# Attention and a two-layer network: matmul operands read alternately from two halves, an unmerged second layer, and a ninth pair transposed by TensorE

## The chip, the cores and the metric

The kernel runs on one core of a Trainium2 chip. The metric is the device time of one execution, in microseconds (us). The kernel before takes 996.13 us (median of three runs, 996.07 to 996.7).

## The reference, cut to what matters

There are 8 batches of 8 heads, 576 positions and 64 values per head. For each head a decayed causal attention is computed, the result is laid out as 4608 tokens of 512 values, and these go through two matrix products with a leaky rectifier between them.

```python
scores = scale * np.matmul(q, k.transpose(0, 1, 3, 2))
cum = np.cumsum(np.log(np.clip(f, 0.0001, 1.0)), axis=-1)
scores = np.where(causal, -1e9, scores + cum[:, :, :, None] - cum[:, :, None, :])
attn = np.exp(scores - scores.max(-1, keepdims=True))
attn = attn / (attn.sum(-1, keepdims=True) + 1e-09)
x = np.matmul(attn, v)            # then reshaped to (4608, 512)
h = x @ w_in                      # (4608, 2048)
g = np.maximum(h, 0.0) + alpha * np.minimum(h, 0.0)
return g @ w_out                  # (4608, 512)
```

## The kernel before, in words

**Order of the work.** The kernel describes its work as some thousands of small operations, each with an engine, an estimated duration, a key, the operations it depends on and the buffers it takes. `Plan.run` (line 136) then simulates the engines: it takes, again and again, the operation that can start first, ties by key, and emits its instructions. The order in each engine's queue is therefore what this planner made of the estimates. The estimates are short functions: `c_mm` (line 325) for one product of n columns, and others for ScalarE, VectorE and GpSimd. Each is multiplied by a random factor between 0.97 and 1.03, drawn from `SEED` (line 27). Attention has small keys and the first layer keys of a million and more, so products of the first layer fill what attention leaves free on TensorE.

**Split operands.** For accuracy most products are done on operands that are split into a high and a low part (type fp32r): high by high, high by low and low by high, three products into one bank, where a full fp32 product would be used otherwise. ScalarE copies the high part, and VectorE or GpSimd subtracts it from the original to get the low part. All products go through the helper `mm` (line 382), so line 383 stands for all of them in the profile; they are told apart by their tiles.

**Attention.** A pair is two heads; there are 32 pairs, 4 per batch. In the profile `Qhl` is the split query and key of a pair; the first four pairs use unsplit `rqk`. Query and key of a pair come from DRAM in one row of 640 + 576 words, made on the host. The exponentials have to be transposed before they are multiplied by the values. For the first `NX` = 8 pairs (line 35) the function `attention` (line 570) does this by TensorE transposes of 128 x 128 blocks (helper `blocks`, line 609) and evacuates them from PSUM. For the others the function `turned` (line 831) uses VectorE transposes of 32 x 32 blocks (line 908) and moves the blocks between partitions by twelve DMAs per pair, six on SP's queue and six on GpSimd's (line 949), and four ScalarE copies (line 946). The decay rows of the first kind of pair come by DMA from DRAM, those of the second kind by two VectorE transposes (lines 515, 517). `quotient` (line 1003) normalizes the result on GpSimd and splits it (lines 1019, 1020) into a block `xx` of the first layer: the first 512 positions of a batch. The last 64 positions of all batches are collected through DRAM (`xt`) as a ninth block.

**First layer.** `ffn1` (line 1046) multiplies: per block and per group of 128 hidden values, four slices of the contraction times three split products of 512 columns, 12 products; 9 x 16 x 12 = 1728. The weights `wi` are split early (`split64`, line 358), and the result goes through the rectifier and to DRAM (`hd`). Each block needs the four pairs of its batch.

**Second layer.** The 4608 tokens are 18 units of 256. `ffn2` (line 1277) computes a unit by a Strassen-like scheme, in which 7 products take the place of 8. The moving operands are split sums of weight quarters (`wot`; the last four of eight lie in the freed `wi`), the stationary ones split sums of the hidden values (`gh`, low parts at line 1321, three buffers). There are 8 slices of the contraction, taken two at a time as groups. For all units but the last (`wide`) three of the seven products are merged: one product of 512 columns takes the high part of the stationary operand against high and low part of the weights side by side, one of 256 takes the low part. Such a unit has 8 x 18 = 144 products and uses five banks; the last one has 8 x 21 = 168 products of 256 columns and four banks. At its end a unit is put together by VectorE adds (lines 1364 to 1371 and 1394) and one ScalarE copy, and stored.

Of the kernel before, what the change touches and what calls it, by code (L numbers as in the profile page):

```python
# [19 lines left out]
NP = H // 2  # L20
# [4 lines left out]
QW = 640  # L25
ZW = 9 * 128
SEED = 66
# [7 lines left out]
NX = 8  # L35
# [14 lines left out]
UNITS = (2, 3, 0, 4, 5, 1, 6, 7, 14, 8, 9, 15, 10, 11, 16, 12, 17, 13)  # L50
NEG = -1.0e30
# [166 lines left out]
def attention_moe(  # L218
# [106 lines left out]
    def c_mm(n):  # L325
        return max(110, 13.3 + 0.4175 * n)
# [4 lines left out]
    def c_row(n, m):  # L331
        return m * max(110, 13.3 + 0.4175 * n)
# [25 lines left out]
    def split64(tiles, src, whi, wlo, key, deps, bufs_out):  # L358
# [21 lines left out]
        return [op("DVE", c_dve(512), lambda: ve.tensor_tensor(wlo(), a().bitcast(F32), whi().bitcast(F32), ALU.subtract), key, [cp], [ba] + bufs_out)]  # L380

# [188 lines left out]
    def attention(n):  # L570
# [11 lines left out]
        nt_ = 3 if n >= NN else 4  # L582
        masks = [o_eye, o_tri] if n < NM else []
# [32 lines left out]
        def tail(st):  # L616
# [4 lines left out]
            for g in range(2):  # L621
# [3 lines left out]
                def prods(bS=bS, ks=ks):  # L625
                    for c, (q, k) in enumerate(terms):
                        mm(bS.t[:, :288], q()[:, 512:640], k()[:, ks], c == 0, c == len(terms) - 1 and not (g and n < NM))
                    if g and n < NM:
                        mm(bS.t[:, 224:288], identb, tri2, False, True)
# [57 lines left out]
        def stretch(tiles, st):  # L687
# [4 lines left out]
            def prods():  # L692
                for i, g, c0 in part:
                    w = 128 * i + 128
                    for c, (q, k) in enumerate(terms):
                        for h in range(2):
                            r = slice(64 * h, 64 * h + 64)
                            mm(bS[g][h].t[:, c0 : c0 + w], q()[r, 128 * i : 128 * i + 128], k()[r, 0:w], c == 0, c == len(terms) - 1 and n >= NM)
# [132 lines left out]
    def turned(n):  # L831
# [22 lines left out]
        def score(i, h, out):  # L854
            r, w = slice(64 * h, 64 * h + 64), 128 * (i + 1)
            return [lambda c=c, q=q, k=k: mm(out(), q()[r, 128 * i : 128 * i + 128], k()[r, 0:w], c == 0, c == 2) for c, (q, k) in enumerate(terms)]
# [63 lines left out]
        def run2():  # L920
            for c0, c1, out in part:
                for c, (q, k) in enumerate(terms):
                    mm(out(), q()[:, 512:640], k()[:, c0:c1], c == 0, c == 2)
# [79 lines left out]
    def quotient(n, bxs, bri, deps, st):  # L1003
# [4 lines left out]
        def scaled():  # L1008
# [10 lines left out]
        xh = op("ACT", c_acs(512), lambda: ac.activation(bx.t[:, 0], bxs.t[:, 0:512], AF.Copy), st, [mu], [bxs, bx])  # L1019
        xl = op("POOL", c_po(512), lambda: po.tensor_tensor(  # L1020
            bx.t[:, 1], bxs.t[:, 0:512], bx.t[:, 0].bitcast(F32), ALU.subtract), st, [xh], [bxs, bx])
# [24 lines left out]
    def ffn1(b):  # L1046

        for fc in range(NF):
            bh, bs = Buf(rH), Buf(rhs)
            last = None  # L1050
            for half in range(2):
                def prods(bh=bh, fc=fc, half=half):
                    for c in (2 * half, 2 * half + 1):
                        x = x_ops[b, c][0].t
                        for k, (wt, m) in enumerate(((0, 0), (0, 1), (1, 0))):
                            mm(bh.t, wi[:, fc, wt, c], x[:, m], c + k == 0, c == NC4 - 1 and k == 2)
# [101 lines left out]
    wot = [None] * (NW - NV) + [wid[:, WN * i : WN * i + WN].rearrange("p (j k n) -> p j k n", k=2, j=7) for i in range(NV)]  # L1158

    def change():  # L1160
# [11 lines left out]
        for i in range(NW - NV):  # L1172
            wot[i] = p1.tile([128, 7, 2, 256], F32R, name=f"wot{i}")
# [33 lines left out]
    for c in range(NC4):  # L1207
        bx = Buf(rx)
        xh = op("ACT", c_acs(512), lambda c=c, bx=bx: ac.activation(bx.t[:, 0], tv()[:, c], AF.Copy), 1e4, [ld[c // 2]], [bt_, bx])
        xl = op("DVE", c_dve(512), lambda c=c, bx=bx: ve.tensor_tensor(  # L1210
            bx.t[:, 1], tv()[:, c], bx.t[:, 0].bitcast(F32), ALU.subtract), 1e4, [xh], [bt_, bx], two=True)
# [10 lines left out]
    def load_w_out(c):  # L1222
# [40 lines left out]
        for j0, j1, d in ((0, 3, done), (3, 7, [su])):  # L1263
            n = 256 * (j1 - j0)
            h = op("ACT", c_acs(n), lambda j0=j0, j1=j1: ac.activation(wot[c][:, j0:j1, 0], bx.t[:, j0:j1], AF.Copy), key, d + base, [bx])
            ready.append(op("DVE", c_dve(n), lambda j0=j0, j1=j1: ve.tensor_tensor(
                wot[c][:, j0:j1, 1], bx.t[:, j0:j1], wot[c][:, j0:j1, 0].bitcast(F32), ALU.subtract), key, [h], [bx], two=True))
# [9 lines left out]
    def ffn2(u):  # L1277

        k0 = 2e6 + 100 * UNITS.index(u)
        wide = u != UNITS[-1]  # L1280
# [6 lines left out]
        for g in range(NW // GW):  # L1287
# [37 lines left out]
            if u == UNITS[-1] and g == NW // GW - 1:  # L1325
                todo = [((cc,), part, 0) for part in (PRODS[:1], PRODS[1:6:4], PRODS[3:5], PRODS[2:3], PRODS[6:]) for cc in range(GW)]
            for m, (ccs, part, k) in enumerate(todo):
                double = part[0][0] in twice

                def prods(part=part, ccs=ccs, k=k, double=double, g=g, bgh=bgh):  # L1330
                    if double:
                        for ia, ib, bank, _ in part:
                            o = bo[4 if ia == 5 else bank].t
                            for cc in ccs:
                                c = GW * g + cc
                                w = wot[c][:, ib]
                                if k == 0:
                                    mm(o, bgh.t[:, 0, ia, cc], w.rearrange("p k n -> p (k n)"), c == 0, False)
                                else:
                                    mm(o[:, 0:256], bgh.t[:, 1, ia, cc], w[:, 0], False, c == NW - 1)  # L1340
# [3 lines left out]
                    for ia, ib, bank, half in part:  # L1344
                        o = bo[bank].t[:, 256 * half : 256 * half + 256]
                        for n, (ka, kb) in enumerate(((0, 0), (0, 1), (1, 0))):
# [3 lines left out]
                            mm(o, bgh.t[:, ka, ia, cc], wot[c][:, ib, kb], first, end)  # L1350
# [100 lines left out]
```

## Time and profile before

| | |
|---|---|
| median of three runs | 996.13 us |
| the profiled execution | 995.95 us |
| its span, first to last instruction | 994.1 us |
| VectorE, busy share of the span | 83% |
| ScalarE, busy share of the span | 67% |
| GpSimd, busy share of the span | 38% |

The span is the time from the first to the last instruction of one execution on the core; the device time is a little longer. Products on TensorE are pipelined: the duration that the profile gives for one overlaps with the next, so that the interval between starts, and not the duration, tells how many fit into a stretch. `PE` is TensorE's matmul, `PEld` its weight load, `DVE` VectorE, `ACT` ScalarE, `POOL` GpSimd, `SP` the queue engine.

### The profile page before, as it was taken

What the parts mean: (1) busy time and instruction counts of PE and PEld (TensorE: products, weight loads), DVE (VectorE), ACT (ScalarE), POOL (GpSimd) and SP (SyncE); (2) the same over time, 40 slices, a digit from 0 to 9 for tenths busy, and PEclk for the clock granted to TensorE, in tenths of its full rate; (3) what the DMA queues carried; (4) which work ended last, traced back from release to release, by engine and by line L of the source; (5) the groups of instructions that cost most, each with busy time, mean ns of one, the idle gap of its engine ahead of it and who ended that gap; (6) DMA issues with size and microseconds to landing.
All of it is one profiled execution on the core that took longest, in us unless ns stands there. A gap on an engine that the chain in (4) does not pass through costs nothing.

```text
span 994.1 us, 20932 instructions
## 1 busy us (share of the span) xinstructions
PE 985.4 (99%) x7462; PEld 860.2 (87%) x7462; DVE 820.7 (83%) x1603; ACT 669.3 (67%) x1382; POOL 376.4 (38%) x598
## 2 busy tenths in 40 slices
PE   9999999999999999999999999999999999999998
PEld 6778878888888888888888888899999999999998
DVE  7877888888878868868655988699999999999994
ACT  7987869998888878779764666563544636454641
POOL 4575675889787867777730100000000000000000
PEclk9999999999999999999999999999999999999999
DMA  7987748788878786868767676533434434344421
GB/s 231 263 240 230 217 125 218 229 233 233 240 224 228 213 226 189 238 193 226 198 173 226 202 222 209 165 130 114 155 121 142 135 129 146 126 132 146 129 86 44
DMA packets 164327, 182.09 MB, mean 183 GB/s; under 512 B 20799, under 2 KB 115806, under 8 KB 164222
## 3 DMA queue, kind: packets, MB, share of 16 engines
q1 hardware_dynamic: 159326, 165.79, 56.6%
q0 software_dynamic: 4608, 14.75, 5.2%
q8 instruction: 59, 0.97, 0.4%
q14 instruction: 46, 0.38, 0.1%
q10 hardware_dynamic: 288, 0.20, 0.1%
HBM read 101.95 MB, written 48.81 MB: 152 GB/s over the span
## 4 chain that ended last, share of the span: by engine, by line
PE 98%; DVE 1%; ACT 1%; issue 0%; POOL 0%; DVEq 0%; POOLq 0%; ACTq 0%
PE bank L383 95%; PE bank L609 2%; PE bank L454 0%; PE bank L488 0%; ACT wi L379 0%; ACT big L605 0%; DVE bank L374 0%; ACT big L596 0%; DVE bank L373 0%; DVE bank L372 0%; PE bank L676 0%; PE bank L750 0%; DVE bank L375 0%; DVE Zt L517 0%; DVE wi L380 0%
## 5 line engine op out<-in xcount | busy, mean ns | idle before, releaser
L383 PE MATMUL bank<-xx,wi 128*128 128x512 f32 x1728 | 404.3, 391 | 1.6 <-ACT wi L379 1.6
L383 PEld LDWEIGHTS bank<-xx,wi 128*128 128x128 f32 x1728 | 320.7, 188 | 68.7 <-ACT wi L379 2.0
L383 PE MATMUL bank<-wot,gh 128*128 128x256 f32 (+1 forms) x1308 | 180.6, 298 | 0.0
L383 PE MATMUL bank<-wi,gh 128*128 128x256 f32 (+1 forms) x1308 | 180.6, 298 | 0.0
L383 PEld LDWEIGHTS bank<-wot,gh 128*128 128x128 f32 x1308 | 169.7, 188 | 9.4
L383 PEld LDWEIGHTS bank<-wi,gh 128*128 128x128 f32 x1308 | 169.6, 188 | 9.3
L851 ACT ACTIVATE big<-big,st 128x512 f32<-128x512 f32 (+4 forms) x216 | 123.8, 575 | 6.2 <-DVE st L871 5.7
L1068 DVE SCALAR_TENSOR_TENSOR hx<-bank,sa,hx 128x512 f32<-128x512 f32 x96 | 70.4, 734 | 61.4 <-ACT hx L1066 61.2
L1066 ACT ACTIVATE hx<-bank,ab 128x512 f32<-128x512 f32 x96 | 65.9, 687 | 55.4 <-PE bank L383 52.4
L908 DVE STREAM_TRANSPOSE big<-big 128x1408 f32<-128x1408 f32 (+2 forms) x72 | 90.5, 1272 | 11.1 <-DMA big<-big 5.1
L383 PEld LDWEIGHTS bank<-big,vr 128*64 128x64 f32 x1888 | 89.1, 137 | 8.8 <-issue 1.9
L383 PE MATMUL bank<-big,vr 128*64 128x128 f32 (+2 forms) x1888 | 95.5, 259 | 1.1 <-DVE st L634 1.1
L563 POOL TENSOR_TENSOR Qhl<-rqk,Qhl 128x640 fp32r<-128x640 f32 (+1 forms) x56 | 83.5, 1505 | 24.9 <-ACT Qhl L562 23.8
L383 PE MATMUL bank<-Qhl 64*128 64x512 f32 (+6 forms) x840 | 92.6, 326 | 0.0
L383 PEld LDWEIGHTS bank<-Qhl 64*128 64x128 f32 (+1 forms) x840 | 75.1, 186 | 15.2 <-issue 9.0
L946 ACT ACTIVATE big<-big 32x800 f32<-32x800 f32 x96 | 83.2, 867 | 5.0 <-DVE big L908 3.9
L949 POOL DMA_DIRECT2D big<-big x144 | 73.0, 512 | 5.6 <-issue 3.7
L535 POOL TENSOR_TENSOR Z<-Z,hx 128x384 f32<-128x384 f32 x60 | 54.9, 924 | 32.2 <-DMA Z<-c 16.0
L1318 ACT ACTIVATE gh<-hg 128x768 fp32r<-128x768 f32 x28 | 23.7, 847 | 62.9 <-PE bank L383 34.2
L871 DVE CUSTOM_DVE_ANT_1 big<-bank,Z 128x384 f32<-128x384 f32 (+1 forms) x96 | 44.7, 486 | 23.6 <-PE bank L383 23.5
L1318 ACT ACTIVATE gh<-wx 128x768 fp32r<-128x768 f32 x28 | 23.7, 847 | 59.3 <-PE bank L383 25.6
L1321 DVE TENSOR_TENSOR gh<-hg,gh 128x1792 fp32r<-128x1792 f32 x28 | 56.5, 2019 | 2.9 <-ACT gh L1320 2.8
(158 smaller groups left out, 1353.5 us busy)
## 6 DMA issues: line engine op xcount, KB each, us to landing
hd<-hx SPq DMA_DIRECT2D x144, 256.0 KB, 3.7
rqk<-in_qk_dram SPq DMA_DIRECT2D x28, 608.0 KB, 5.0
big<-big SPq DMA_DIRECT2D x144, 100.0 KB, 4.8
big<-big POOLq DMA_DIRECT2D x144, 100.0 KB, 4.6
hg<-hd SPq DMA_DIRECT2D x28, 512.0 KB, 4.2
wx<-hd SPq DMA_DIRECT2D x28, 512.0 KB, 4.2
vr<-in_vv_dram SPq DMA_DIRECT2D x32, 320.0 KB, 4.6
big<-in_w_in_dram SPq DMA_DIRECT2D x16, 512.0 KB, 5.7
```

Source lines behind the costliest of these rows:

```text
L383: pe.matmul(o, lhsT, rhs, start=start, stop=stop)
L535: m1 = op("POOL", c_po(128 * 3), lambda z4=z4: po.tensor_tensor(z4()[:, 6:9], z4()[:, 0:3], tb(3), ALU.add), kc + 0.1, got + [o_mask], [bZ])
L563: o2 = op("POOL", c_po(w), lambda hi=hi, lo=lo, raw=raw: po.tensor_tensor(lo(), raw(), hi().bitcast(F32), ALU.subtract), kc, [o1], [bqk, bQ])
L851: sums.append(op("ACT", c_exp(w), lambda: ac.activation(at(), at(), AF.Exp, bias=lo()[:, col : col + 1], scale=-1.0, accum_out=su()[:, col ...
L871: ve.tensor_tensor_reduce(out=blk(e()), in0=blk(src()), in1=in1, scale=-0.125, scalar=3.0e38, op0=ALU.add, op1=ALU.min, accum_out=lo()[:, ...
L908: ve.transpose(t_t[:, :, c0 : c0 + 32 * (b1 - b0)].rearrange("p k (b c) -> p k b c", c=32), bE.t[:, 128 * off : 128 * (off + b1 - b0)].rea ...
L946: moves.append(op("ACT", c_acs(CW), lambda a=a: ac.activation(bM.t[32 * a : 32 * a + 32, a], t_t[32 * a : 32 * a + 32, a, 32 * TA * bTa.i ...
L949: moves.append(op(n_, 550 if i % 2 else 450, lambda a=a, k=k, q_=q_: q_.dma_start(bM.t[32 * k : 32 * k + 32, a], t_t[32 * a : 32 * a + 32, ...
L1066: cp = op("ACT", c_act(512), lambda bh=bh, bs=bs, fc=fc: ac.activation(bs.t, bh.t, AF.Relu, scale=ab[:, fc : fc + 1]), -1000, [last, o_sg] ...
L1068: cp = op("DVE", c_dve(512), lambda bh=bh, bs=bs, fc=fc: ve.scalar_tensor_tensor(bs.t, bh.t, sa[:, fc : fc + 1], bs.t, ALU.mult, ALU.add), ...
L1318: h0 = op("ACT", c_acs(3 * 128 * GW), lambda bhx=bhx, bgh=bgh: ac.activation(bgh.t[:, 0, 0:3], bhx.t[:, 1:4], AF.Copy), key, o1, [bhx, bgh])
L1321: his, rdy = [h0, h1], [op("DVE", c_tt(7 * 128 * GW), lambda bhx=bhx, bgh=bgh: ve.tensor_tensor(bgh.t[:, 1], bhx.t[:, 1:8], bgh.t[:, 0].bi ...
```

## The change

A helper `weave` returns a view of columns c0 to c1 in which consecutive columns come by turns from the first and the second half of a tile. Every split product now reads its moving operand through it: scores of pairs 4 to 31, first layer, second layer. So that the result stays in its order, the even columns are stored in the first half and the odd ones in the second: on the host for the keys (`qk1`), and in the instructions that split the operands of both layers, which read every second word. In the second layer no unit merges products any more (`WIDE` is empty): each has 168 products of 256 columns in four banks, the last group's order of the former last unit, and another end. `NX` is 9, so pair 8 is transposed by TensorE. The planner's estimate `c_mm` and its seed are other ones.

```diff
-SEED = 66
+SEED = 6
-NX = 8
+NX = 9
+WIDE = ()
     def c_mm(n):
-        return max(110, 13.3 + 0.4175 * n)
+        return max(112, 2.5 + 0.4167 * n)
     def c_row(n, m):
-        return m * max(110, 13.3 + 0.4175 * n)
+        return m * c_mm(n)
+    def weave(t, c0, c1):
+        return t.rearrange("p (a n) -> p n a", a=2)[:, c0 // 2 : c1 // 2]
# attention(n)
+        cols_of = weave if n >= NN else lambda t, c0, c1: t[:, c0:c1]
-                        mm(bS.t[:, :288], q()[:, 512:640], k()[:, ks], ...)
+                        mm(bS.t[:, :288], q()[:, 512:640], cols_of(k(), 288 * g, 288 * g + 288), ...)
-                            mm(bS[g][h].t[:, c0 : c0 + w], q()[r, 128 * i : 128 * i + 128], k()[r, 0:w], ...)
+                            mm(bS[g][h].t[:, c0 : c0 + w], q()[r, 128 * i : 128 * i + 128], cols_of(k()[r], 0, w), ...)
# turned(n): score and run2 in the same way, with weave
# quotient
-        xh = op("ACT", c_acs(512), lambda: ac.activation(bx.t[:, 0], bxs.t[:, 0:512], AF.Copy), ...)
+        halves = lambda m: bx.t[:, m].rearrange("p (a n) -> p a n", a=2)
+        turns_of = lambda: bxs.t[:, 0:512].rearrange("p (n a) -> p a n", a=2)
+        xh = op("ACT", c_acs(512), lambda: ac.activation(halves(0), turns_of(), AF.Copy), ...)
         xl = op("POOL", c_po(512), lambda: po.tensor_tensor(
-            bx.t[:, 1], bxs.t[:, 0:512], bx.t[:, 0].bitcast(F32), ALU.subtract), ...)
+            halves(1), turns_of(), halves(0).bitcast(F32), ALU.subtract), ...)
# ffn1 (and the ninth block's split in the same way as quotient's)
-                            mm(bh.t, wi[:, fc, wt, c], x[:, m], ...)
+                            mm(bh.t, wi[:, fc, wt, c], weave(x[:, m], 0, 512), ...)
# load_w_out
+            part = lambda k, j0=j0, j1=j1: wot[c][:, j0:j1, :, k]
+            src = lambda j0=j0, j1=j1: bx.t[:, j0:j1].rearrange("p j (n a) -> p j a n", a=2)
-            h = op("ACT", ..., ac.activation(wot[c][:, j0:j1, 0], bx.t[:, j0:j1], AF.Copy), ...)
+            h = op("ACT", ..., ac.activation(part(0), src(), AF.Copy), ...)
-                wot[c][:, j0:j1, 1], bx.t[:, j0:j1], wot[c][:, j0:j1, 0].bitcast(F32), ALU.subtract), ...)
+                part(1), src(), part(0).bitcast(F32), ALU.subtract), ...)
# ffn2
-        wide = u != UNITS[-1]
+        wide = u in WIDE
-            if u == UNITS[-1] and g == NW // GW - 1:
+            if not wide and g == NW // GW - 1:
-                            mm(o, bgh.t[:, ka, ia, cc], wot[c][:, ib, kb], first, end)
+                            mm(o, bgh.t[:, ka, ia, cc], wot[c][:, ib, :, kb].rearrange("p a n -> p n a"), first, end)
-        e1 = op("DVE", c_tt(256), ... bo[3].t[:, :256] + bs.t[:, 3] ...)
-        for i, k in ((0, 2), (4, 4)):
-            e1 = op("DVE", 2 * c_tt(256), lambda i=i, k=k: both(i, k), ...)
+        if wide:
+            ...
+        else:
+            e1 = op("DVE", c_tt(512), lambda: ve.tensor_tensor(bs.t[:, 0:5:4], two(bo[2].t), rep(3), ALU.add), ...)
# host
+    qkrow1 = np.concatenate([qrow, krow[..., 0::2], krow[..., 1::2]], axis=-1)
-        "qk1": qkrow.reshape(...)
+        "qk1": qkrow1.reshape(...)
```

## Rows read from the trace of the kernel before

**Rows 1.** Page, parts 1 and 2: busy time by engine; granted TensorE clock in 40 slices.

```profile
PE 985.4 (99%) x7462; PEld 860.2 (87%) x7462; DVE 820.7 (83%) x1603; ACT 669.3 (67%) x1382; POOL 376.4 (38%) x598
...
PEclk9999999999999999999999999999999999999999
```

**Rows 2.** Chain of waits that ended last: start us, length us, what; two of its pieces.

```profile
137.00 0.50 ACT wi L379
...
142.42 847.81 PE bank L383 x6270
```

**Rows 3.** Windows: us, busy us (xinstructions) of each engine, PEclk, DMA share, GB/s.

```profile
150.00:200.00 50.00, 50.00 (x411) 42.36 (x410) 42.75 (x101) 45.42 (x111) 36.33 (x60) 1.00 0.80 227
...
550.00:600.00 50.00, 50.00 (x222) 41.41 (x221) 43.96 (x75) 31.63 (x47) 0.85 (x1) 1.00 0.78 230
700.00:750.00 50.00, 50.00 (x366) 47.17 (x365) 47.25 (x63) 25.63 (x39) 0.00 (x0) 1.00 0.42 134
```

**Rows 4.** Groups by shape on TensorE: names, shapes xcount | busy us, mean ns | idle before.

```profile
L383 PE MATMUL bank<-xx,wi 128*128 128x512 f32 x1728 | 404.3, 391 | 1.6 <-ACT wi L379 1.6
...
L609 PE MATMUL bank<-big 128*128 128x128 f32 x192 | 27.9, 276 | 0.7 <-ACT big L605 0.7
```

**Rows 5.** Timeline of TensorE in six stretches: start us, us, what xcount (consecutive ones merged).

```profile
122.53 0.93 PE L609 MATMUL bank<-big 128*128 128x128 f32 x7
123.29 0.27 PE L750 MATMUL bank<-big 128*64 128x128 f32 x1
...
308.16 2.19 PE L383 MATMUL bank<-Qhl 64*128 64x512 f32 x24
310.29 2.99 PE L383 MATMUL bank<-big,vr 128*64 128x128 f32 x60
...
528.58 1.66 PE L383 MATMUL bank<-xx,wi 128*128 128x512 f32 x6
...
539.82 60.45 PE L383 MATMUL bank<-xx,wi 128*128 128x512 f32 x266
...
634.80 5.56 PE L383 MATMUL bank<-wot,gh 128*128 128x512 f32 x38
...
970.27 10.06 PE L383 MATMUL bank<-wot,gh 128*128 128x256 f32 x84
980.17 10.05 PE L383 MATMUL bank<-wi,gh 128*128 128x256 f32 x84
```

**Rows 6.** Tile gh: TensorE's second-layer products, duration ns min/median/max, first and last start.

```profile
L383 PE MATMUL bank<-wi,gh x1308: 278/280/397, 644.7 to 989.9; 128*128 128x256 f32 x158, 128*128 128x512 f32 x29
```

**Rows 7.** Groups by shape of TensorE's weight loads (PEld), columns as in Rows 4.

```profile
L383 PEld LDWEIGHTS bank<-xx,wi 128*128 128x128 f32 x1728 | 320.7, 188 | 68.7 <-ACT wi L379 2.0 <-DVE wi L380 0.7 <-issue 0.7
...
L609 PEld LDWEIGHTS bank<-big 128*128 128x128 f32 x192 | 22.0, 141 | 7.0 <-ACT big L605 1.7 <-ACT big L596 0.7 <-issue 0.7
```

**Rows 8.** Groups by shape on VectorE, 650 to 950 us: result sums, low parts.

```profile
L1364 DVE TENSOR_TENSOR hx<-bank,hx 128x256 f32<-128x256 f32 x61 | 24.5, 422 | 2.5
...
L1367 DVE TENSOR_TENSOR hx<-bank,hx 128x512 f32<-128x512 f32 x15 | 10.4, 692 | 1.6
...
L1394 DVE TENSOR_TENSOR hx<-bank,hx 128x256 f32<-128x256 f32 x16 | 6.7, 417 | 0.1
```

**Rows 9.** Groups on ScalarE, VectorE and GpSimd, whole execution: copies and subtractions of splits.

```profile
L1019 ACT ACTIVATE xx<-hx 128x512 fp32r<-128x512 f32 x32 | 19.6, 623 | 2.6 <-PE bank L383 1.3 <-POOL hx L1013 1.0
...
L1239 ACT ACTIVATE wx<-wr 128x512 f32<-128x512 f32 x16 | 10.4, 666 | 0.0
...
L1243 DVE SCALAR_TENSOR_TENSOR wx<-wr,wx 128x512 uint32<-128x512 uint32 x16 | 11.1, 693 | 0.5
...
L1020 POOL TENSOR_TENSOR xx<-hx,xx 128x512 fp32r<-128x512 f32 x32 | 42.1, 1322 | 25.2 <-ACT xx L1019 23.0 <-issue 1.7
```

**Rows 10.** Page, part 5: the transposed pairs on VectorE and on GpSimd's queue.

```profile
L908 DVE STREAM_TRANSPOSE big<-big 128x1408 f32<-128x1408 f32 (+2 forms) x72 | 90.5, 1272 | 11.1 <-DMA big<-big 5.1
...
L949 POOL DMA_DIRECT2D big<-big x144 | 73.0, 512 | 5.6 <-issue 3.7
```

More of the change, by code (lines that the diff above doesn't have):

```diff
@@ L626, in prods @@
                     for c, (q, k) in enumerate(terms):
-                        mm(bS.t[:, :288], q()[:, 512:640], k()[:, ks], c == 0, c == len(terms) - 1 and not (g and n < NM))
+                        mm(bS.t[:, :288], q()[:, 512:640], cols_of(k(), 288 * g, 288 * g + 288), c == 0, c == len(terms) - 1 and not (g and n < NM))
                     if g and n < NM:
@@ L697, in prods @@
                             r = slice(64 * h, 64 * h + 64)
[L698 removed]
+                            mm(bS[g][h].t[:, c0 : c0 + w], q()[r, 128 * i : 128 * i + 128], cols_of(k()[r], 0, w), c == 0, c == len(terms) - 1 and n >= NM)
                     for j in range(2 if n < NM else 0):
@@ L855, in score @@
             r, w = slice(64 * h, 64 * h + 64), 128 * (i + 1)
-            return [lambda c=c, q=q, k=k: mm(out(), q()[r, 128 * i : 128 * i + 128], k()[r, 0:w], c == 0, c == 2) for c, (q, k) in enumerate(terms)]
+            return [lambda c=c, q=q, k=k: mm(out(), q()[r, 128 * i : 128 * i + 128], weave(k()[r], 0, w), c == 0, c == 2) for c, (q, k) in enumerate(terms)]
         def both(i, out):
@@ L1157, in attention_moe @@
     WN = 7 * 2 * 256
-    wot = [None] * (NW - NV) + [wid[:, WN * i : WN * i + WN].rearrange("p (j k n) -> p j k n", k=2, j=7) for i in range(NV)]
+    wot = [None] * (NW - NV) + [wid[:, WN * i : WN * i + WN].rearrange("p (j a k n) -> p j a k n", a=2, k=2, j=7) for i in range(NV)]
     def change():
@@ L1393, in ffn2 @@
             return
-        e1 = op("DVE", c_tt(256), lambda: ve.tensor_tensor(bs.t[:, 3], bo[3].t[:, :256], bs.t[:, 3], ALU.add), -500, [e0], [bo[3], bs])
-        for i, k in ((0, 2), (4, 4)):
-            e1 = op("DVE", 2 * c_tt(256), lambda i=i, k=k: both(i, k), -500, [e1, ends_of[-5]], [bo[k], bs])
-        e1 = op("DVE", c_tt(512), ends, -500, [e1, ends_of[-3]], [bo[1], bs])
+        if wide:
+            e1 = op("DVE", c_tt(256), lambda: ve.tensor_tensor(bs.t[:, 3], bo[3].t[:, :256], bs.t[:, 3], ALU.add), -500, [e0], [bo[3], bs])
+            for i, k in ((0, 2), (4, 4)):
+                e1 = op("DVE", 2 * c_tt(256), lambda i=i, k=k: both(i, k), -500, [e1, ends_of[-5]], [bo[k], bs])
+        else:
+            e1 = op("DVE", c_tt(512), lambda: ve.tensor_tensor(bs.t[:, 0:5:4], two(bo[2].t), rep(3), ALU.add), -500, [e0, ends_of[-7]], [bo[2], bs])
+        e1 = op("DVE", c_tt(512), ends, -500, [e1, ends_of[-3 if wide else -5]], [bo[1], bs])
         e2 = op("DVE", c_tt(512) + c_tt(256), ends2, -500, [e1, last], [bo[0], bo[1], bs])
```

30 lines of the change are left out of this document (16 added, 14 removed).

## The prediction

> **What bounds the kernel now.** I read part 1 of the page first: TensorE is busy 985.4 us of a span of 994.1 us, and the granted clock is full in every slice [rows 1], so neither the clock nor idle time explains the time. The chain of waits says the same from the other end: from 142.42 us to the end it is one unbroken run of 6270 products, 847.81 us long; before that there are short pieces of the first layer's weight splitting, such as the ScalarE copy of line 379 at 137.00 us [rows 2]. So after 142 us the time is the number of products times the interval between their starts. The windows say who would be next: from 150 to 200 us ScalarE has 45.42 of 50 us and VectorE 42.75, from 550 to 600 us VectorE 43.96, and from 700 to 750 us, in the second layer, VectorE 47.25 with TensorE at 50.00 [rows 3].
>
> The durations of products (391 ns [rows 4]) overlap, so I take intervals from starts. First layer alone: 266 products in 60.45 us, the last one lasting 0.39, is 60.06/265 = 226.6 ns each for 512 columns [rows 4, 5]. Second layer without merging (the last unit): 84 products from 970.27 to 980.17 us, 117.9 ns each for 256 columns [rows 5]. Columns alone, at the granted 2.4 GHz, would be 213.3 and 106.7 ns. The excess is 13.3 ns at 512 and 11.2 ns at 256: nearly a constant per product, not a share of the columns. The fp32 transposes, with 128 columns and one weight load of 128 columns each, start every (123.29 - 122.53)/7 = 108.6 ns [rows 5]. So 108.6 ns is what one load per product costs at the least; 256 columns lie just under it. The loads themselves last 188 ns beside first-layer products and 141 ns in the transposes [rows 7]: something makes a load slower where split words are read in a row at one word per column. That is the place that the new order of reading touches. It is a hint and no proof, since every moving operand of the trace runs through at least 32 consecutive words.
>
> **The change, part by part.**
>
> *Interval of a first-layer product.* 1728 products at 226.6 ns [rows 4, 5]. The trace has no product that reads alternately, so I bound it: at best 213.3 ns (columns alone), at worst a word each two column times, 426.7 ns; no change is 226.6. The planner's own price line helps to choose: the old one, 13.3 + 0.4175 n, gives 227.1 and 120.2 ns where the trace has 226.6 and 117.9, so such lines are within 2% of the chip. The new one, 2.5 + 0.4167 n, gives 215.8. I take 215.8: 1728 x 10.8 = 18.7 us less; best end 23.0 us less; no change 0; worst end in the rival below.
>
> A page of the Trainium skill speaks against this. SBUF — State Buffer, section "Door 1: The DMA port swizzle", says that lines of 16 bytes give full bandwidth only from the second access in a row to the same line, and that each crossing to another line pays. Reading two halves by turns crosses at every word. No row here tests it; by it the sum would be that of the last rival, by the rows on loads the one below.
>
> *Second layer.* It runs from 634.80 to the last start at 989.9 us [rows 5, 6]: 355.1 us for 2616 products (17 units of 144, in which three of seven products are merged into one of 512 and one of 256 columns, and a last one of 168). Afterwards 18 x 168 = 3024 products of 256 columns. The interval lies between 108.6 (the transposes' load) and 117.9 ns (no gain); the new price line has a floor of 112. I take 110.5, nearer to the load row: 334.2 us, 20.9 us less. Ends: 108.6 gives 328.4 (26.7 less), 112 gives 338.7 (16.4 less), 117.9 gives 356.5 (1.4 more: the merging lost with nothing for it).
>
> VectorE must keep up. Beside TensorE's 50.00 us it has 47.25 [rows 3], 2.75 us per 50 spare. The unmerged ending drops, per unit, four adds of 422 ns and one of 417 for one of about 692 [rows 8]: 1.4 us less of some 19.7 us. Faster products take (355.1 - 334.2)/18 = 1.2 us off a unit. So VectorE's share stays what it was, and it hid before; I charge 0. Unmerged, a group's first product waits also for the low parts of line 1321, which the merged first product did not; behind it stand all products of the group in TensorE's order. Three buffers keep VectorE ahead. If that cover were gone, about 1 us per unit, 18 us, would come back. Four banks per unit instead of five let the next unit start in four free ones; no row shows TensorE waiting for a bank, so 0.
>
> *Scores.* One pair's score products run from 308.16 to 310.29 us: 24 records, two heads side by side, 3 x (512 + 384 + 256 + 128) columns [rows 5]. Columns, with 108.6 as the floor of the two short ones, are 3 x (213.3 + 160 + 108.6 + 108.6) = 1.77 us; they took 2.13. Of the 0.36 us part is the start-up after a product of another kind. I take 0.18 x 28 pairs = 5.0 us less; ends 0 and 10.
>
> *Ninth pair by TensorE.* 192 transposes in 8 pairs [rows 4] are 24 more at 108.6 ns: 2.6 us, with the sums' turn and separate score stretches 3.0 us more on the path; nothing if they fall into TensorE's 8.7 us of idle [rows 1], 5 if each stretch starts slowly. It frees VectorE of three transposes of 1272 ns and GpSimd's queue of six issues of 512 ns [rows 10], and SP's of six as well; it adds row copies from DRAM on SP in place of two more VectorE transposes, ahead of the later loads there, and evacuations on ScalarE. None of these engines is on the chain after 142 us, so 0; before it, they are part of the next term.
>
> *Strided sides.* The splits now read every second word. ScalarE reading so takes 666 ns (line 1239) where line 1019 takes 623 in a row; VectorE reading so takes 693 for 512 words (line 1243), no more than an add in a row (692, line 1367) [rows 8, 9]. 33 + 4 copies at 43 ns more and 16 larger ones are under 4 us of ScalarE, spread over 600 us and off the chain: 0, at most 4 if ScalarE is full from 150 to 200 us. GpSimd's subtraction at 1322 ns [rows 9] has no strided row; if it took half as much again, 33 x 0.66 = 22 us of an engine under 40% busy [rows 1]: 0 on the path.
>
> *Reserve of work.* The last attention product ends about 528.58 us, and 634.80 - 528.58 = 106.2 us of first layer follow: 469 products. Of these 2 x 192 need the last four pairs and could not go earlier; 85, or 19.3 us, are TensorE's reserve. By then it saves 1259 x 10.8 = 13.6 plus 5.0, less 3.0 for the pair: 15.6 us. The reserve just covers it, if attention on the other engines keeps its pace. Before 142 us TensorE waits for weight splitting [rows 2], and what its products save there is partly given back. I charge 4 us; ends 0 and 13. The other seed reorders the plan by jitter of 3% in its costs: nothing by itself, give or take 3 us.
>
> *Sum.* 994.1 - 18.7 - 20.9 - 5.0 + 3.0 + 4.0 = 956.5 us of span. The profiled execution took 995.95 us, 1.85 above its span, and lies 0.18 below the median of 996.13; so 956.5 + 1.85 + 0.2 = 958.6 us.
>
> **The rivals.**
>
> *Half.* The excess shrinks only by half: 9.4 us in the first layer, (117.9 + 110.5)/2 = 114.2 ns in the second (345.3 us, 9.8 less), 2.5 in scores, plus 3 and 3: 994.1 - 15.7 + 2.05 = 980.5 us. The same time comes if VectorE or attention gives back 22 us. For it: VectorE at 47.25 of 50 [rows 3]. Against: it loses work too.
>
> *No gain.* The excess belongs to the product itself and not to the order of its words: 1.4 + 3.0 more, 1000.6 us. For it: the excess hardly grows with columns. Against: loads differ by 47 ns between kinds of reading [rows 7], so it is not one fixed cost.
>
> *Slower.* Each word read from the other half pays for a new place. If it halves the supply: 512 columns in 426.7 + 2, 202 ns more on 1728 products, 349 us; 3024 products at 215.3 are 651 us, 296 more; scores some 45. That is 1689 us. It decides from small sizes on: the sum's 37.6 us are gone once the products, some 372.9 + 334.2 + 60 us after the change, take 5% longer; a tenth of the halving would end near 1032. For it: such reading has no row, and every product of both layers would pay. The Trainium skill's page SBUF — State Buffer would have it so. Against: only the planner's new price line, which its forerunner's closeness to the trace makes likely.
>
> **How the numbers follow.** Forecast 0.72, with its own range 945 to 972: best ends of the terms together would be 936, which I leave out, and the losses' ends add 9 and 4. Half 0.09, no gain 0.07, slower 0.12. Range 945 to 988 takes in the forecast and the half: 0.80. Within 0.2% of 996 is about what a measurement can tell from no change. No gain lies 0.4% above; of its 0.07 I count 0.02 as same. Faster 0.81, same 0.02, slower 0.17.
>
> **What would show it.** In the first layer alone, products of 512 columns every 215 to 217 ns; in the second, 3024 products, 84 of them in 9.1 to 9.5 us; weight loads nearer to 141 ns than 188. VectorE still below TensorE there. TensorE without idle from 150 us on, or idle near 530 us if the reserve fell short. Intervals at or above 226.6 and 117.9 would make the prediction wrong, and so would TensorE idle of 10 us and more.

## The result and the profile after

The changed kernel takes 961.07 us (median of 4 runs, 959.44 to 962.38), the kernel before 996.25 us beside it: ratio 0.9645, 95% interval 0.9629 to 0.9662. The forecast was 958.6 us. The profiled execution took 962.38 us, its span is 960.6 us, 33.5 less than before. Of these, 17.1 are gone when the second layer starts (634.80 us before [rows 5], 617.69 now) and 16.5 more at its last start (355.1 us of second layer before [rows 5, 6], 338.6 now).

From the page of the changed kernel, the busy times by engine, which answer [rows 1]:

```profile
PE 950.5 (99%) x7908; PEld 866.2 (90%) x7908; DVE 801.6 (83%) x1529; ACT 684.5 (71%) x1389; POOL 370.4 (39%) x589
```

TensorE still has 99% of the span, with 446 more instructions in 33.5 us less. So the time went where the products follow one another, and the timeline of TensorE (start us, us, what, xcount of consecutive ones) shows it; these lines answer [rows 5]:

```profile
307.11 2.07 PE L388 MATMUL bank<-Qhl 64*128 64x512 f32 x24
309.11 2.99 PE L388 MATMUL bank<-big,vr 128*64 128x128 f32 x60
...
516.14 2.98 PE L388 MATMUL bank<-big,vr 128*64 128x128 f32 x60
...
529.73 60.49 PE L388 MATMUL bank<-xx,wi 128*128 128x512 f32 x279
...
937.68 9.54 PE L388 MATMUL bank<-wot,gh 128*128 128x256 f32 x84
947.06 9.54 PE L388 MATMUL bank<-wi,gh 128*128 128x256 f32 x84
```

In the first layer 279 products, the last lasting 0.38, are (60.49 - 0.38)/278 = 216.2 ns each where there were 226.6. In the second, 84 take 947.06 - 937.68 = 9.38 us, 111.7 ns each where there were 117.9. One pair's scores take 2.00 us instead of 2.13.

The windows answer [rows 3] (us, busy us and instructions of PE, PEld, DVE, ACT, POOL, clock, DMA share, GB/s), and one line of TensorE's waits stands behind them (us in total, times, longest):

```profile
550.00:600.00 50.00, 50.00 (x233) 43.53 (x232) 47.47 (x70) 37.24 (x48) 0.00 (x0) 1.00 0.75 215
650.00:700.00 50.00, 49.19 (x441) 49.00 (x440) 48.81 (x62) 26.90 (x40) 0.00 (x0) 1.00 0.46 147
700.00:750.00 50.00, 50.00 (x450) 50.00 (x450) 46.54 (x58) 24.63 (x36) 0.00 (x0) 1.00 0.45 137
```

```profile
PE bank L388 <- DVE gh L1333: 0.8, 1, 0.8
```

VectorE has 46.54 of 50 us in the second layer, 47.25 before; at the start of that layer it reaches 48.81, and there TensorE waits once for the low parts of the hidden values (line 1333, line 1321 before), 0.8 us. That is all that VectorE takes back. The weight loads (mean ns after the busy us) answer [rows 7]:

```profile
L388 PEld LDWEIGHTS bank<-xx,wi 128*128 128x128 f32 x1728 | 322.1, 189 | 46.0 <-DVE st L877 0.8 <-issue 0.3 <-DVE xx L1220 0.2
L388 PEld LDWEIGHTS bank<-wot,gh 128*128 128x128 f32 x1512 | 170.4, 192 | 0.1
...
L615 PEld LDWEIGHTS bank<-big 128*128 128x128 f32 x216 | 25.0, 141 | 7.9 <-ACT big L611 2.4 <-ACT hx L789 1.1 <-issue 0.7
```

They last 189 and 192 ns, as long as before, although the products come faster. Their duration was no sign of the loss.

### The profile page after: what moved, and what is told of

It is laid out like the page before. It is cut to its first block, busy times and chain, and to the rows that moved or that the text cites. A ratio compares the mean times of both kernels' runs of the same rounds, so it can differ in the third digit from the quotient of the medians.

```text
span 960.6 us, 21712 instructions
## 1 busy us (share of the span) xinstructions
PE 950.5 (99%) x7908; PEld 866.2 (90%) x7908; DVE 801.6 (83%) x1529; ACT 684.5 (71%) x1389; POOL 370.4 (39%) x589
## 4 chain that ended last, share of the span: by engine, by line
PE 88%; DMA 4%; DVE 4%; ACT 1%; SPq 1%; issue 1%; POOL 0%; DVEq 0%; ACTq 0%
PE bank L388 86%; PE bank L615 2%; DMA big<-big 1%; DMA rqk<-in_qk_dram 1%; DMA big<-in_w_in_dram 1%; DVE hx L1076 1%; DMA hd<-hx 1%; DVE gh L1333 1%; SPq L955 1%; DMA hx<-rd 0%; DVE big L914 0%; ACT hx L1074 0%; DVE big L877 0%; DVE Z L520 0%; ACT big L602 0%
## 5 line engine op out<-in xcount | busy, mean ns | idle before, releaser
L388 PE MATMUL bank<-xx,wi 128*128 128x512 f32 x1728 | 384.9, 381 | 0.6 <-DVE st L877 0.6
L388 PE MATMUL bank<-wi,gh 128*128 128x256 f32 x1512 | 172.0, 275 | 0.8 <-DVE gh L1333 0.8
L388 PE MATMUL bank<-wot,gh 128*128 128x256 f32 x1512 | 171.8, 275 | 0.0
L857 ACT ACTIVATE big<-big,st 128x384 f32<-128x384 f32 (+4 forms) x207 | 118.5, 575 | 7.5 <-DVE st L877 4.5
L914 DVE STREAM_TRANSPOSE big<-big 128x1408 f32<-128x1408 f32 (+2 forms) x69 | 87.8, 1279 | 16.9 <-ACT big L857 7.5
L388 PE MATMUL bank<-Qhl 64*128 64x512 f32 (+6 forms) x840 | 88.2, 318 | 0.2 <-DVE hx L1076 0.2
L952 ACT ACTIVATE big<-big 32x800 f32<-32x800 f32 x92 | 79.7, 866 | 6.6 <-DVE big L914 5.7
L955 POOL DMA_DIRECT2D big<-big x138 | 69.6, 510 | 3.2 <-issue 2.0
L1333 DVE TENSOR_TENSOR gh<-wx,gh 128x1792 fp32r<-128x1792 f32 x26 | 52.4, 2017 | 0.0
L1028 POOL TENSOR_TENSOR xx<-hx,xx 128x512 fp32r<-128x512 f32 x32 | 41.5, 1304 | 27.6 <-ACT xx L1027 26.5
```

What stands on the lines that cost most here:

```text
L388: pe.matmul(o, lhsT, rhs, start=start, stop=stop)
L857: sums.append(op("ACT", c_exp(w), lambda: ac.activation(at(), at(), AF.Exp, bias=lo()[:, col : col + 1], scale=-1.0, accum_out=su()[:, col ...
L914: ve.transpose(t_t[:, :, c0 : c0 + 32 * (b1 - b0)].rearrange("p k (b c) -> p k b c", c=32), bE.t[:, 128 * off : 128 * (off + b1 - b0)].rea ...
L952: moves.append(op("ACT", c_acs(CW), lambda a=a: ac.activation(bM.t[32 * a : 32 * a + 32, a], t_t[32 * a : 32 * a + 32, a, 32 * TA * bTa.i ...
L955: moves.append(op(n_, 550 if i % 2 else 450, lambda a=a, k=k, q_=q_: q_.dma_start(bM.t[32 * k : 32 * k + 32, a], t_t[32 * a : 32 * a + 32, ...
L1028: xl = op("POOL", c_po(512), lambda: po.tensor_tensor(halves(1), turns_of(), halves(0).bitcast(F32), ALU.subtract), st, [xh], [bxs, bx])
```

## The experiments

Two theories stood at first. *Reading*: the order in which the moving words are read sets the interval, and the rest of the change lives from that. *Rest*: the unmerged second layer, the ninth pair and the other order of the plan carry a good part of it. Then, of the reading itself: does the excess lie in where the two words are, in the meeting with the weight load, or elsewhere. Each ratio below is to runs of the kernel before on the same chip.

**The changed kernel, read in a row.** Everything stays but the alternate reading; the splits and the host write in a row again.

```diff
     def weave(t, c0, c1):
-        return t.rearrange("p (a n) -> p n a", a=2)[:, c0 // 2 : c1 // 2]
+        return t[:, c0:c1]
```

> The changed kernel with one thing undone: every product reads its moving operand in a row again, and the splits write in a row; the planner's order, the ninth pair, the unmerged second layer and the prices stay. Theory (the order of reading carries the gain): first-layer products back at 226.6 ns (1728 x 10.7 = 18.5 us), second-layer products at 117.9 (3024 x 6.1 = 18.4 us), scores 3.6 us: span 960.6 + 40.5 = 1001, time near 1003 us. Rival (the new plan, the ninth pair and the unmerged second layer carry it): 961 to 975 us.

It took 999.11 us (10 runs, 997.31 to 1000.04; before 996.71), ratio 1.0023 (1.0013 to 1.0033). Its timeline of TensorE, a stretch of the first layer and two of the second:

```profile
549.63 40.74 PE L388 MATMUL bank<-xx,wi 128*128 128x512 f32 x179
...
973.05 9.96 PE L388 MATMUL bank<-wot,gh 128*128 128x256 f32 x84
982.85 9.96 PE L388 MATMUL bank<-wi,gh 128*128 128x256 f32 x84
```

The intervals are (40.74 - 0.39)/178 = 226.7 and 9.80/84 = 116.7 ns. The sum had said near 1003. Without the reading the rest of the change costs 2.4 us; *rest* is refuted as a gain of its own.

**The kernel before with the alternate reading alone.** The second layer merges as before, eight pairs, the old estimate and seed.

```diff
# against the changed kernel
-SEED = 6
+SEED = 66
-NX = 9
+NX = 8
-WIDE = ()
+WIDE = UNITS[:-1]
-        return max(112, 2.5 + 0.4167 * n)
+        return max(110, 13.3 + 0.4175 * n)
```

> The kernel before with alternate reading alone: eight pairs, merged products, old prices and old seed, so the planner's order of before. Theory, TensorE alone: 18.5 us less in the first layer, 408 merged products 16.8 ns shorter and 2208 others 6.1 ns shorter in the second (20.3 us), 3.6 in scores: span 951.7, time near 953.7. Theory with VectorE as the next bound of the merged second layer (some 345 us of VectorE against 335 us of TensorE there): 960 to 966 us, with TensorE idle in the second layer. Rival (the plan and not the reading): 990 to 997 us.

973.32 us (972.71 to 973.95), ratio 0.9763 (0.9749 to 0.9778): 23.4 us of some 35 come from reading alone. That is 7 us over the range expected with VectorE as the bound: its second layer takes 351.5 us, 3.6 less than before, where 345 was taken. The waits of TensorE and a window of the second layer:

```profile
PE bank L388 <- DVE gh L1333: 9.5, 8, 1.4
PE bank L388 <- DVE hx L1407: 3.6, 5, 0.8
```

```profile
700.00:750.00 50.00, 47.82 (x369) 45.64 (x368) 48.30 (x66) 22.71 (x32) 0.00 (x0) 1.00 0.41 127
```

VectorE has 48.30 us of the 50 and TensorE 47.82, waiting for low parts and for the sums of a unit's end. With merged units faster products meet VectorE as the next bound.

**The changed kernel, merged again,** and **with five merged units.** One constant each.

```diff
-WIDE = ()
+WIDE = UNITS[:-1]          # the other kernel: WIDE = (3, 5, 7, 9, 11)
```

> The changed kernel with the second layer's products merged again in 17 units; reading by turns, ninth pair, prices and seed stay. Theory (VectorE is the bound of a merged second layer): that layer takes 351 us as with alternate reading on the old plan, in place of 338.6; time 961 + 12 = 973 us, with TensorE waiting for VectorE there. Rival (TensorE alone): a merged pair of products takes 215.9 + 111.7 ns in place of 3 x 111.7, 24 times per unit, 0.18 us x 17 = 3.1 us less: 958 us.

> The changed kernel with five of 18 units merged, one in each stretch of three. Theory: VectorE has some 2.6 us to spare in a stretch of three units and a merged unit takes 1.4 us of it, so TensorE gains 5 x 0.18 = 0.9 us: 960.1 us. Rival (VectorE's spare time is used up by its order): 961 to 966 us.

All units but one merged: 977.01 us (974.59 to 977.53), ratio 0.9797 (0.9781 to 0.9813), second layer 354.2 us. Five merged: 960.83 us (959.79 to 962.0), ratio 0.9641 (0.9627 to 0.9656), second layer 339.6 us, no different from none. The first one's largest wait of TensorE and its window:

```profile
PE bank L388 <- DVE gh L1333: 15.2, 7, 2.6
```

```profile
700.00:750.00 50.00, 48.17 (x375) 46.22 (x374) 48.37 (x66) 22.71 (x31) 0.00 (x0) 1.00 0.41 128
```

So unmerging is worth 15.9 us here; read in a row, the whole rest of the change was worth nothing (unmerging alone, read in a row, was not run). It adds 408 products and takes adds from VectorE; that pays only once the products are so fast that VectorE would set the pace, and a few merged units can still hide.

**The kernel before with reading and unmerging,** without the ninth pair, the new estimate and seed.

```diff
# against the changed kernel
-SEED = 6
+SEED = 66
-NX = 9
+NX = 8
-        return max(112, 2.5 + 0.4167 * n)
+        return max(110, 13.3 + 0.4175 * n)
```

> Reading by turns and the unmerged second layer with eight pairs, the old prices and the old seed: all but the ninth pair, prices and seed. Theory (unmerging frees VectorE, and the rest of the change is worth little once the reading is there): the second layer starts at 615 us, as with the merged one on this plan, takes 338.6 and 4.2 us of ending: span 958, time 960 us, the same as the changed kernel. Rival (the ninth pair and the new plan are needed for the gain): 965 to 973 us.

962.12 us (959.33 to 963.31), ratio 0.9648 (0.9632 to 0.9663): as fast as the changed kernel, with TensorE full in the second layer. So the 35 us are 23.4 from reading and 11.2 from unmerging on top of it; what the other three edits do together lies within the spread.

```profile
700.00:750.00 50.00, 50.00 (x450) 50.00 (x450) 46.18 (x57) 25.66 (x39) 0.00 (x0) 1.00 0.45 147
```

**Seed and ninth pair.** Three kernels, each the changed one with the constants shown.

```diff
-SEED = 6
+SEED = 66                  # old_seed
-NX = 9
+NX = 8                     # eight_pairs
-SEED = 6, NX = 9
+SEED = 27, NX = 8          # eight_pairs_27
```

> The changed kernel with the seed of before, 66, in place of 6. Prediction's claim: the seed is worth at most 3 us: 958 to 964 us. Rival after the run with eight pairs, which was 27 us slower than its count of products: under the new prices the order that the planner finds depends on the seed, and TensorE runs out of work between 130 and 530 us: 968 to 980 us.

> The changed kernel with eight pairs by TensorE's transposes in place of nine; the planner orders anew. Theory of the sum: 24 transposes and their company, 3 us less on TensorE: 958 us. Rival (the ninth pair relieves VectorE and the DMA queues, and pays for itself): 961 to 966 us, with more TensorE idle between 130 and 530 us.

> The changed kernel with eight pairs, as in the run that took 988.7 us, and another seed (27). If eight pairs under the new prices are slow by themselves: 980 to 990 us. If that run's order was one unlucky draw of the planner: 960 to 972 us.

Old seed: 962.74 us (959.43 to 963.43), ratio 0.9652 (0.9636 to 0.9667), the same as the changed kernel. Eight pairs: 988.68 us (987.75 to 989.65), ratio 0.992 (0.9906 to 0.9935), 27 us worse and far outside both expectations. Eight pairs with another seed: 963.64 us (962.88 to 963.98), ratio 0.9668 (0.9652 to 0.9685). So the 27 us belong to one order of the plan and not to the pair. In the kernel with eight pairs and seed 6, TensorE's waits and two windows of attention:

```profile
PE bank L388 <- POOL xx L1028: 7.5, 5, 2.2
PE bank L388 <- ACT wi L380: 3.9, 2, 3.1
```

```profile
100.00:150.00 50.00, 45.00 (x395) 36.91 (x394) 41.36 (x89) 35.59 (x93) 33.24 (x44) 0.97 0.54 155
...
200.00:250.00 50.00, 46.70 (x389) 40.23 (x388) 35.87 (x84) 38.42 (x86) 36.58 (x60) 0.93 0.71 201
```

TensorE stands still for blocks that are not split yet, while VectorE, ScalarE and GpSimd from 200 to 250 us are less busy than in the changed kernel (42.10, 46.00 and 41.29 us there). The granted clock of these windows is 0.97 and 0.93 of 2.4 GHz beside the waits, so part of them ran at the lower level, 1.2 GHz. Counted in the two traces with eight pairs: TensorE's waits sum to 22.8 us with seed 6 and 9.3 with seed 27; 27 products of the first layer start every 427 ns and 26 of the second every 213 without a wait, 8.3 us above the usual interval (1.5 us with seed 27). So of the 24.3 us between the two spans the waits are the greater part, 13.5 us, and products at the lower clock some 7.

**How the reading order sets the interval.** Two kernels, the one before with the last two blocks of the first layer read in another way per four groups of hidden values, 48 products each. READ gives a pattern for each kind.

```diff
# ffn1
-                            mm(bh.t, wi[:, fc, wt, c], x[:, m], ...)
+                            kind = (b - 7) * 4 + fc // 4
+                            r = lambda t: t.rearrange(*READ[kind])   # in a row: t
+                            mm(bh.t[0:cut], wi[:, fc, wt, c, 0:cut], r(x[:, m]), ...)
# halves "p (a n) -> p n a" a=2; step 2 "p (n a) -> p a n" a=2; quarters a=4;
# two words of each half "p (a n t) -> p n a t" t=2; 16 bytes apart "p (k a n) -> p k n a" n=4
```

> The kernel before, in which the first layer's last two blocks read in eight ways, 48 products each, so tokens of these blocks come out in another order and in two stretches some products use half the weights: a row (226.6 ns), two halves by turns, even words and then odd words (step of two words), four quarters by turns, two words from each half by turns, words 16 bytes apart by turns, a row with weight loads of 64 instead of 128 columns in 7 of 12 products, halves by turns with such loads. If leaving the row is what counts: 216 ns for all but the rows. If each jump to another line of 16 bytes paid, alternate reading would be slow, 16 bytes apart slowest, pairs and the step of two near 227. If only far alternation helps: 216 for halves and quarters, 227 for the step of two, for pairs and for 16 bytes apart. If the excess is the meeting of a weight load with reading in a row: halved loads give 226.6 - 13.3 x 7/24 = 222.7; if it is a fixed price of the product, 226.6.

> The kernel before, in which the first layer's last two blocks read in eight other ways, 48 products each (tokens of these blocks come out in another order). Hypothesis from the first such run: odd and even words of a product are fetched as two streams; a stream that takes four words in a row from a line of 16 bytes costs nothing, two words little, one word much. It gives: halves by turns, each with a step of two words, 227 ns; words 8 bytes apart by turns 227; words 32 bytes apart by turns 216; four words from each half by turns 227; eight by turns 227; a step of four words 453; quarters by turns, two at a time, 216; a row 227. Rival (any reading by turns between two places is free, and any step is not): 216 for words 8 bytes apart, 453 for halves with a step of two, 216 for four and eight words by turns.

Their times (1009.67 and 1009.15 us, one execution each) say little by themselves, since the slow stretches set them. The timeline of TensorE in the first kernel, in this order: in a row; halves by turns; every second word, then the others (step 2); quarters by turns; two words of each half by turns; 16 bytes apart by turns; in a row, and halves by turns, both with loads of 64 columns in 7 of 12 products:

```profile
547.37 11.27 PE L383 MATMUL bank<-xx,wi 128*128 128x512 f32 x49
558.25 10.53 PE L383 MATMUL bank<-xx,wi 128*128 128x512 f32 x48
568.83 21.92 PE L383 MATMUL bank<-xx,wi 128*128 128x512 f32 x48
590.58 13.30 PE L383 MATMUL bank<-xx,wi 128*128 128x512 f32 x48
603.72 16.16 PE L383 MATMUL bank<-xx,wi 128*128 128x512 f32 x48
619.71 10.53 PE L383 MATMUL bank<-xx,wi 128*128 128x512 f32 x48
630.07 11.20 PE L383 MATMUL bank<-xx,wi 128*128 128x512 f32 x48
641.12 10.52 PE L383 MATMUL bank<-xx,wi 128*128 128x512 f32 x48
```

From start to start, over the 48 products of each kind, these are 226.7, 215.8, 453.0, 273.8, 333.1, 215.9, 230.1 and 215.8 ns (a line of 49 has one product of its neighbour). Two things follow. Half of the load doesn't lower the 226.7 (230.1 came, and why it is longer stays open), so the excess is not a meeting of the words with the weight load. And two places 16 bytes apart do as well as two halves of the tile: what counts is that two places come by turns, one word each, and they need not be far apart. In the second kernel, five of the eight: 8 bytes apart by turns; 32 bytes apart; four words of each half by turns; eight words; quarters by turns, two at a time:

```profile
559.52 11.04 PE L383 MATMUL bank<-xx,wi 128*128 128x512 f32 x48
570.63 10.52 PE L383 MATMUL bank<-xx,wi 128*128 128x512 f32 x48
580.99 12.17 PE L383 MATMUL bank<-xx,wi 128*128 128x512 f32 x48
592.99 11.84 PE L383 MATMUL bank<-xx,wi 128*128 128x512 f32 x48
...
626.27 11.00 PE L383 MATMUL bank<-xx,wi 128*128 128x512 f32 x49
```

That is 226.7, 215.8, 250.0, 243.3 and 216.2 ns, so 8 bytes apart is too near. The other three: halves with step 2 in each 226.7, step 4 459.7, in a row 227.3. My picture from the first kernel was that odd and even words of the order come as two streams, and a stream is free if it finds four consecutive words in a row, pays some 11 ns per product if it finds two (as in a row), and double if one. It gave six of the eight, but not the turns of four and eight words, where it said 227 and 250.0 and 243.3 came. So the order of reading as the cause of the 10.8 ns is shown; the two streams are a guess that fits most orders and not all, and how the words are fetched stays open. The rival (any turns of two places are free, any step is not) missed in four.

The order also has a price on other engines, which the first of these kernels shows. One of ScalarE's instructions (line 1244 there) reads every second word of 1024. These ran beside the row, beside halves by turns, and beside words 16 bytes apart by turns:

```profile
549.58 1.23 ACT L1244 ACTIVATE wx<-wr 128x512 f32<-128x512 f32 x2
...
562.10 1.67 ACT L1244 ACTIVATE wx<-wr 128x512 f32<-128x512 f32 x2
...
625.73 0.66 ACT L1244 ACTIVATE wx<-wr 128x512 f32<-128x512 f32 x1
```

One by one they take 667 and 662 ns, then 882 and 907, then 662. VectorE's reads of every second word (lines 1248 and 1251) take 684 to 693 beside the row, 814 to 884 beside the halves, and 691 and 693 beside 16 bytes apart; in the second kernel, beside 32 bytes apart, ScalarE takes 662 and 667. So turns 16 bytes apart, with the same 215.9 ns, would spare the other engines this; no run used them in the whole kernel, and why halves cost it stays open.

**What bounds the second layer.** The changed kernel, with the products of five units changed one way each: in units 6, 12 and 14 the second and third of three split products, but for each bank's last, in units 8 and 10 all of them.

```diff
# ffn2, by the unit's place in UNITS
-                            mm(o, bgh.t[:, ka, ia, cc], r, first, end)   # r: halves by turns
+        6: mm(o[0:64], bgh.t[:, ka, ia, cc, 0:64], r, ...)       # half loads
+        8: r in a row        10: r quarters by turns
+        12, 14: mm(o[:, 0:2*cut], bgh..., r[:, 0:cut], ...)      # 128, 224 columns
```

> The changed kernel, in which some units of the second layer leave out or reorder work: one with weight loads of 64 columns in two of three split products, one reading in a row, one reading four quarters by turns, one with 128 columns and one with 224 columns in two of three split products instead of 256. Theory that the load of 128 columns sets the 111.8 ns of a product of 256 columns: half loads bring two of three products to 109.2 or less (mean 110.1), 224 columns change nothing (111.8), 128 columns little (108 to 111.8), in a row 117.9. Rival, columns plus a fixed price of 5 ns: half loads 111.8, 224 columns 98, 128 columns 58 in these products.

It took 967.54 us (one execution). TensorE's timeline, two lines for each unit (its two weight tiles): half loads, in a row, quarters, 128 columns, and an unchanged unit:

```profile
730.57 9.40 PE L388 MATMUL bank<-wot,gh 128*128 128x256 f32 x84
739.81 9.41 PE L388 MATMUL bank<-wi,gh 128*128 128x256 f32 x84
...
767.82 9.97 PE L388 MATMUL bank<-wot,gh 128*128 128x256 f32 x84
777.63 9.96 PE L388 MATMUL bank<-wi,gh 128*128 128x256 f32 x84
...
806.18 12.19 PE L388 MATMUL bank<-wot,gh 128*128 128x256 f32 x84
818.21 12.21 PE L388 MATMUL bank<-wi,gh 128*128 128x256 f32 x84
...
849.01 9.49 PE L388 MATMUL bank<-wot,gh 128*128 128x256 f32 x84
858.34 9.60 PE L388 MATMUL bank<-wi,gh 128*128 128x256 f32 x84
...
905.29 9.54 PE L388 MATMUL bank<-wot,gh 128*128 128x256 f32 x84
914.67 9.54 PE L388 MATMUL bank<-wi,gh 128*128 128x256 f32 x84
```

From start to start, over 84, they are 110.0, 116.8, 143.2, 111.1 and 111.7 ns. Half the columns in two of three products don't make them faster (the whole unit has 111.7 as well, and so has the one of 224 columns); loads of half the width do, to 109 ns for the products that have them (these also write half the partitions; the two were not separated). So with alternate reading the weight load, and not the columns, sets a product of 256 columns at 111.7 ns; read in a row, the columns set it at 116.8.

## Why the prediction was right, and where it was off

*What bounds.* "After 142 us the time is the number of products times the interval between their starts" held: reading in a row gives the whole gain back, and no other engine bounds the result.

*The terms, in us of span.* I add up each product's time to the next start, by kind, in both traces.

| term | predicted | measured |
|---|---|---|
| first layer, 1728 products | -18.7 | -21.8 (400.6 to 378.8) |
| second layer | -20.9 | -16.5 (355.1 to 338.6) |
| scores | -5.0 | -3.6 (86.7 to 83.1) |
| ninth pair's transposes | +3.0 | +3.1 (23.2 to 26.3) |
| reserve, other products, waits | +4.0 | +5.3 |
| sum | -37.6 | -33.5 |

*The first layer* was right in its interval (215.8 predicted, 216.2 measured: 1728 x 10.4 = 18.0 us). Most of the rest of the 21.8 lies before 150 us, where this layer's products took 5.3 us above 226.7 ns each in the kernel before and 2.5 us above 215.8 now. That is the new plan and not the reading: with the reading alone the layer takes 382.8 us, 17.8 less. The prediction had the number from the planner's new price line and no mechanism for it. The one place that it named, a load that is slower beside words read in a row, was wrong: half loads did not shorten the row (230.1), and the loads last as long as before. So the price line was a good witness, and the warning of the Trainium skill was not: its page SBUF — State Buffer, section "Door 1: The DMA port swizzle", would have each crossing to another 16-byte line pay. The runs disagree where two places come by turns (215.8, less than the 226.7 in a row) and agree that some other orders are dear (273.8 for four places). The page would have a step of up to four fp32 words free; here a step of two took 453.0.

*The second layer is the mis-sized step*: I wrote "I take 110.5, nearer to the load row" and 111.7 came, 112.0 with waits, 4.4 us in all. The net miss is 4.1 us; that the other terms cancel, 3.1 us better in the first layer and 2.8 worse in the rest, is luck. The direction of that step was right and is now shown: a load of 128 columns is the bound. But the transposes' 108.6 ns was the wrong row for it, and the price line's floor of 112, which I listed as an end, was the right one. That I took a value between two ends with a mechanism behind only one of them is the fault.

*VectorE* "hid before; I charge 0": right, 0.8 us of waits. It was nearer than the sum told: merged units would have cost 15.9 us. My comparison of shares (1.4 us less work, 1.2 us less time) was the part that mattered, and it held only because the change did both. The end in one add is 687 ns (692 forecast):

```profile
L1411 DVE TENSOR_TENSOR hx<-bank,hx 128x512 f32<-128x512 f32 x16 | 11.0, 687 | 9.0 <-ACT gh L1332 9.0
```

*Strided sides.* ScalarE's and GpSimd's lines, in the two splits of a block, answer [rows 9]. The third line is line 1239 of before, whose instruction the change leaves alone:

```profile
L1027 ACT ACTIVATE xx<-hx 128x512 fp32r<-128x512 f32 x32 | 24.3, 779 | 0.1
...
L1028 POOL TENSOR_TENSOR xx<-hx,xx 128x512 fp32r<-128x512 f32 x32 | 41.5, 1304 | 27.6 <-ACT xx L1027 26.5 <-issue 0.6
...
L1249 ACT ACTIVATE wx<-wr 128x512 f32<-128x512 f32 x16 | 14.3, 914 | 0.0
```

The same instruction in the changed kernel read in a row:

```profile
L1245 ACT ACTIVATE wx<-wr 128x512 f32<-128x512 f32 x16 | 10.4, 661 | 0.0
```

ScalarE's split of every second word takes 779 ns where 623 were, not 666. Line 1239 was a fair neighbour for the step itself, but it was read beside products in a row: beside the halves by turns it takes 914. So more of the price seems to come from the reading beside it than from the step, and the prediction had no such term; the split with a step beside a row was not run. GpSimd takes 1304 where 1322 were. TensorE waited for neither.

*Reserve and order.* "The reserve just covers it" was not put to the test. The sum let attention end when it had ended before, so that faster products would use up the reserve. But attention came forward: its last products end at 519.05 us (528.58 before), and 456 products of the first layer follow where 468 did. With the reading alone they end at 513.05 us, 15.5 earlier, and 468 follow. TensorE was out of work for little, 48.62 of 50 us busy from 350 to 400 us. The charge of 4 us came to 5.3, but for other things: 2.5 are products that only fill early waits (16 more of them, line 493) and 1.4 idle time. That it lies so near is luck. The sign "TensorE idle of 10 us and more" named no stretch: over the whole span it was idle 10.1 us (8.7 before), from 150 us to its last product 2.3. "Give or take 3 us" for the seed was right for the two seeds of the change, which differ by nothing measurable, and wrong as a bound: one seed with eight pairs cost 27 us.

*The hint on loads* was wrong as a sign: they were to come "nearer to 141 ns than 188" and stayed at 189 and 192, while the interval fell. A duration of an overlapped instruction told nothing about the bound.

*The rivals.* *No gain* and *slower* fell with the first interval. *Half* gave a time not reached, but its second door, VectorE, is real: that is the kernel with reading alone, 973.32 us.

## What to carry to other kernels

Where a long run of products has no gaps, take the interval from starts and ask what stands above the columns; the order in which moving words are read can be a part of it, and a view alone changes it. When products get faster, ask which engine becomes the next bound before valuing a second edit: read in a row, unmerging and the other edits together were worth nothing; beside the new reading unmerging was worth 11 to 16 us. Look also at instructions that a change leaves alone: reading faster on one engine can slow the reads of another. A planner's order can be worth as much as an edit, so an edit is to be judged with more than one seed.

## What the runs showed of the hardware

- A split (fp32r) product of 512 columns whose moving words come by turns from two places takes 215.8 ns, in a row 226.7, by a step of two words 453.0, and from four places by turns 273.8, but 216.2 if these come two at a time.
- Two places 8 bytes apart are as slow as a row (226.7), 16 or 32 bytes apart as good as two halves (215.9, 215.8).
- With alternate reading, one weight load of 128 columns per product holds products of 256, 224 and 128 columns at a mean of 111.7 ns; one of 64 columns lets those of 256 have 109.
- One instruction of ScalarE that reads every second word (512 of 1024) takes 662 to 667 ns beside products read in a row or 16 bytes apart by turns, and 882 and 907 beside halves by turns; VectorE's go from 684 to 693 up to 814 to 884.
- GpSimd's subtraction takes 1304 ns with every second word, 1322 in a row.
